# Mask lists copied on chip, values loaded alone, weight loads tied to GpSimd: one change to an mLSTM and mixture-of-experts kernel

## The chip, the cores and the metric

The kernel runs on one core of a Trainium2 chip. The metric is the device time of one launch in microseconds. The time before is the median of three runs. One more execution was recorded by the hardware profiler; every row below comes from it.

## What is computed

Two layers follow each other. The first is a recurrent attention (mLSTM) over 4 batches, 8 heads, 768 positions and 40 features per head; the second sends its output, as 3072 tokens of 320 features, through eight experts with four slots each.

```python
# first layer, for each position t
m_new = maximum(f_gate[t] + m, i_gate[t])
f_stab, i_stab = exp(f_gate[t] + m - m_new), exp(i_gate[t] - m_new)
C = f_stab * C + i_stab * outer(v[t], k[t])
n = f_stab * n + i_stab * k[t]
y[t] = sigmoid(o_gate[t]) * (C @ q[t]) / maximum(abs(n . q[t]), 1)

# second layer, x = y as 3072 x 320
logits = x @ phi                                  # 3072 x 32
d = softmax(logits, over tokens);  c = softmax(logits, over slots)
slot_input = d.T @ x                              # 8 experts x 4 slots x 320
slot_out[e] = maximum(slot_input[e] @ w1[e], 0) @ w2[e]
out = c @ slot_out
```

## The kernel before, in words

The sequence is cut into 6 chunks of 128 positions. A step is one chunk of one batch, so there are 24 steps, ordered chunk by chunk; four steps of one chunk are a group. Everything is written out in program order: each engine executes its instructions in exactly the order in which the code issues them, and waits on semaphores where a tile is not ready. All transfers are issued on SyncE (SP), in one queue, in program order too; a transfer that has to wait for its tile holds back every later one.

For each step the kernel makes three things on TensorE. `expo` (L271 in chunk 0, L273 later) builds the exponents of the decay between all pairs of positions as a product of two lists: `LB` on the left and `RB` on the right, 128 partitions each. Partitions 0 to 63 and those with ones are the fixed part of a list (a triangular mask and selectors); 12 partitions of RB and 24 of LB hold the gate sums of the chunk. There are two buffers of each, one for odd chunks and one for even ones. ScalarE then takes the exponential (L279) and copies the last column as the keys' decay `rl` (L282). `scores` (L293) multiplies queries and keys, `qc` (L307) multiplies queries with the state C, and ScalarE copies that out of its bank as `qs` (L310). `pv` (L363) multiplies decayed scores with values and `state` (L345, L346) decayed keys with values. Banks are scarce: `qc` and `state` share the single bank `ps`, so the products of `state` wait until `qs` is copied.

GpSimd scales the state (`decay_c`, L325), the keys (`keys`, L331: the keys' decay), the outputs (`gate`, L392, tile x) and qs (`decay_q`, L319). VectorE multiplies decay and scores (`mix`, L298) and prepares the denominators (L380 to L383). TensorE turns x (`xtr`, L409), and with some lag the logits and slot sums of finished groups are accumulated.

The loop body of step i issues work ahead: `load_kv(i + 3)`, `load_w1`, `load_wave`, `expo(i + 2)`, `scores(i + 1)`, `qc(i + 1)`, `load_qk(i + 4)`, `keys(i + 1)`, `gate(i - 1)`, `decay_q(i + 1)`, `pv(i)`, `state(i)`. A KV tile holds the keys (320 columns) and the values with a constant column (328). The keys are used by `keys`, which returns at once from step 20 on, since the state after the last chunk isn't needed. No KQ or KV is loaded by steps 21 and 22, no KQ by step 20.

The gate sums of chunks 2 to 5 are worked out in steps 0 to 3, a few operations a step (`emit(rest, RP[i])`, at the end of a step). In step 2 these are L204 and L205 on VectorE, the cast L215 on ScalarE and L216 on GpSimd; in step 3 the cast L217 on ScalarE and L218 on GpSimd. They are then written to memory (`put_gates`, step 4) and read back into the lists (`get_gates`). The fixed part of the odd lists is loaded at the start by `static(1)`, that of the even ones by `static(0)` in step 2.

The weights of the experts come as 20 blocks of w1 (128 x 1024, 512 KB), one a step from step 3 on, and 16 waves of w2 (128 x 4 x 320, 640 KB). A wave goes into tiles of the first layer that are no longer used: wave 0 in step 21, waves 1 and 2 in step 22, the rest behind the loop, as the tiles come free. `W1N` and `W2N` give the numbers by step. In step 21 GpSimd also clears the tiles for the slots (`slT`, `hT`, L640). Behind the loop `up` (L719) multiplies the slots with w1 and `down` (L745) with w2, wave by wave; `combine` (L763) writes the output.

Of the kernel before, what the change touches and what calls it, by code (L numbers as in the profile page):

```python
# [14 lines left out]
B, H, S, D = 4, 8, 768, 40  # L15
# [3 lines left out]
NSTEP = B * NCH  # L19
DM = H * D  # L20
# [3 lines left out]
GRP = B  # L24
# [27 lines left out]
NKV = 4  # L52
NKQ = 3
NX = 7
NWARM = 9
W1N = (0, 0, 0, 1, 1, 1, 1, 1, 1, 1, 1, 1, 1, 1, 1, 1, 1, 1, 1, 1, 1, 1, 1)
W2N = {21: 1, 22: 2}
KT = 128 // 2
KG = KT + 3 * B
# [7 lines left out]
def kernel(ctx: ExitStack, tc: tile.TileContext, qk, kv, og, g0, g1, g2, masks, consts, cr, cl, w1, w2, *outs):  # L67
# [3 lines left out]
    V, A, G, T = nc.vector, nc.scalar, nc.gpsimd, nc.tensor  # L71
# [6 lines left out]
    def pmt(shape, name, tag="pm"):  # L78
        return pp.tile(shape, F32, tag=tag, name=name, bufs=2 if tag == "pm" else 1)

    def load(dst, src):
        nc.sync.dma_start(dst, src)  # L82
# [12 lines left out]
    KV = [KV2[n // 2][:, n % 2] for n in range(NKV)]  # L95
    KQ_ = [sb.tile([P, 1280], F32, tag=f"KQ{n}", name=f"KQ{n}") for n in range(NKQ)]
    KQ = [t[:, 0:1024].rearrange("p (u j t) -> p u j t", u=2, j=4) for t in KQ_]
    RB = [sb.tile([P, 2, 4, L], BF16, tag=f"RB{n}", name=f"RB{n}") for n in range(2)]
    LB = [sb.tile([P, 2, B, L], BF16, tag=f"LB{n}", name=f"LB{n}") for n in range(2)]
# [34 lines left out]
    w1_sb, w2_sb, run = {}, {}, {}  # L134
    NL = NSTEP - 1

    def load_qk(i):
        if i < NSTEP:
            load(KQ[i % NKQ], qk[i])

    def load_kv(i):
        if i < NSTEP:
            load(KV[i % NKV], kv[i])

    def load_sig(gi, u):
        if gi < NGRP:
# [4 lines left out]
    def load_w1(n=1):  # L151
        for _ in range(n):
            k = len(w1_sb)
            if k < 20:
                w1_sb[k] = sb.tile([P, 4 * DM if k == 0 else FF], F32, tag=f"w1_{k}", name=f"w1_{k}")[:, 0:FF]
                load(w1_sb[k], w1v[:, k, :])

    waves = [("w2r0", 1), ("w2r1", 1), ("w2r2", 1), ("sig", 2), ("KQ0", 1), ("KQ1", 1), ("KV0", 1), ("ew", 3),
# [2 lines left out]
    def load_wave(n=1):  # L161
        for _ in range(n):
            w = len(w2_sb)
            tag, bufs = waves[w]
            t = sb.tile([P, 4, DM], F32, tag=tag, name=f"w2_{w}", bufs=bufs)
            load(t, w2[w])
            w2_sb[w] = [t[:, j] for j in range(4)]
# [10 lines left out]
    def static(n):  # L178
        load(RB[n].rearrange("p r j t -> p (r j t)"), cr)
        load(LB[n].rearrange("p a b s -> p (a b s)"), cl)  # L180
# [6 lines left out]
    def gates_of(lo, hi):  # L187
        t, o = (gf1, L) if lo < 2 * L else (gf2, 2 * L)
        return t[:, 0, lo - o:hi - o], t[:, 1, lo - o:hi - o]
# [36 lines left out]
    def put_gates(c0, c1):  # L226
        for u in range(2):
            load(W[u, 3 * c0 - 3:3 * c1 - 3].rearrange("q r t -> r q t"),
                 gp[32 * u:32 * u + 32, c0 - 1:c1 - 1].rearrange("p c q t -> p (c q) t"))

    def get_gates(c):
        if c >= NCH:
            return
        n = c % 2
        load(RB[n][KT:KG].rearrange("p r j t -> p (r j t)"), W[0, 3 * c - 3:3 * c].rearrange("q (b h) t -> (q b) (h t)", b=B))
        load(LB[n][KG:KA].rearrange("p a b s -> p a (b s)"),
             W[1, 3 * c - 3:3 * c].rearrange("q (h b) t -> (q h) (b t)", b=B).unsqueeze(1).broadcast_to([3 * H, 2, B * L]))

    def turn_g(c0, c1):
        pd = pmt([P, c1 - c0, 2, NS], f"pdec{c0}")  # L240
        for c in range(c0, c1):
            x = gates_of(c * L, c * L + L)[1][0:NS]
            T.transpose(pd[:, c - c0, 0], x, ident[0:NS, 0:NS])
            T.matmul(pd[:, c - c0, 1], x[:, L - 1:L].broadcast_to([NS, P]), ident[0:NS, 0:NS], start=True, stop=True)
        A.activation(dec[:, c0 - 1:c1 - 1], pd, AF.Exp)
# [54 lines left out]
    def qc(i):  # L300
        if i < B or i >= NSTEP:
            return
        t, b = KQ[i % NKQ], i % B
        pqs[i] = pq = pp.tile([P, 4, 2, V1], F32, tag="ps", name=f"pq{i}")
        for j in range(4):
            for a in range(2):
                T.matmul(pq[64 * a:64 * a + 64, j].rearrange("p u d -> p (u d)"), t[:, 0, j, 64 * a:64 * a + 64],  # L307
                         C_[:, b, j].rearrange("p u d -> p (u d)"), start=True, stop=True)
        qs[i] = sb.tile([P, 4, 2, V1], F32, tag="qs", name=f"qs{i}", bufs=2)
        A.copy(qs[i], pq)  # L310
# [16 lines left out]
    def keys(i):  # L327
        if i >= NSTEP - B:
            return
        t = kr[i] = KR[i % 2]  # L330
        G.tensor_tensor(  # L331
            t[:, 24:24 + DM].rearrange("p (j r d) -> p j r d", j=4, r=2),
            KV[i % NKV][:, 0:DM].rearrange("p (j r d) -> p j r d", j=4, r=2),
            rl[i].rearrange("p r j -> p j r").unsqueeze(3).broadcast_to([P, 4, 2, D]), ALU.mult)
# [135 lines left out]
    def exp_e():  # L470
        A.activation(run["e"], run["e"], AF.Exp)
# [34 lines left out]
    def sigm(gi):  # L506
        if gi < NGRP:
            A.activation(sig[gi], sig[gi], AF.Tanh, scale=0.5)
# [31 lines left out]
    for i in range(NSTEP - 1):  # L540
        gm, ph_ = divmod(i - 1, GRP)
        gm -= 1
        live = gm >= 0
        if i == 0:
            load_qk(3)
        load_kv(i + 3)
        if i == 0:
            put_gates(1, 2)
            get_gates(1)
        if i == 2:  # L550
            static(0)
        if i == 4:
            put_gates(2, NCH)
            get_gates(2)
        if i % GRP == 2 and i > 2:
            get_gates(i // GRP + 2)
        if i < len(W1N):
            load_w1(W1N[i])
        load_wave(W2N.get(i, 0))

        expo(i + 2)
        if live and ph_ == 1:
            ex_dT(gm)
        if live and ph_ == 2:
            exp_e()
        if live and ph_ == 3:
            comb_hi()
        decay_c(i)
        scores(i + 1)
        qc(i + 1)  # L570
        load_qk(i + 4)
        if i % GRP < 2:
            load_sig(i // GRP + 1, i % GRP)
        if i % GRP == 3:
            sigm(i // GRP + 1)
        keys(i + 1)
        gate(i - 1)
        decay_q(i + 1)
        if i == NL - 1:
            run["x23"] = sb.tile([P, DM + 1], F32, tag="dec", name="x23")  # L580
            G.memset(run["x23"][:, DM:DM + 1], 1.0)
        mix(i + 1)
        if live and ph_ == 2:
            norm_e(gm)
        if live and ph_ == 3:
            comb_lo(G)
        pv(i)
        state(i)
        if i == 0:
            A.activation(sig[0][:, 0], sig[0][:, 0], AF.Tanh, scale=0.5)  # L590
        if i == 1:
            A.activation(sig[0][:, 1:], sig[0][:, 1:], AF.Tanh, scale=0.5)
        if live and ph_ == 0:
            pl = pmt([P, P], f"pl{gm}")
            logits_mm(gm, pl, range(GRP))
            ex_lt(gm, pl)
        if live and ph_ == 1:
            if i == NL - 1:
                pv(NL, "ps")
                psT = pp.tile([P, 2, 512], F32, tag="psc", name="psT")  # L600
                peT = pp.tile([P, 2, 512], F32, tag="pe", name="peT")
            turn_d(gm)
            xtr(i - 1)
            if i < NL - 1:
                pd = pmt([P, GRP, NS], f"pd2{gm}")
                T.transpose(pd.rearrange("p j s -> p (j s)"), run["lt"], ident)
        if live and ph_ == 2:
            psl = slots(gm)
        ops = post_ops(i)
        emit(ops, int(i >= B))  # L610
        carry(i)
        emit(ops)
        if live and ph_ == 0:
            emit(top_ops(gm, run["lt"]))
        if live and ph_ == 1 and i < NL - 1:
            emit(e0_ops(gm, pd))
        if live and ph_ == 2:
            add_slots(gm, psl)
        if i == NL - 1:
            gate(NL - 1)  # L620
            emit(post_ops(NL))
            for h0 in (0, 4):
                gate(NL, V, h0, h0 + 4)
        if not (live and ph_ == 1):
            xtr(i - 1)
        if live and ph_ == 3:
            comb_h(gm, comb_T(pmt([P, GRP, P], f"pc{gm}")))
        if i < len(RP):
            emit(rest, RP[i])
        if i == 0:  # L630
            G.tensor_copy(run["identr"], ident)
        if i == 1:
            turn_g(1, 2)
        if i == 4:
            turn_g(2, NCH)
        if i == NL - 2:
            slT = [sb.tile([P, n, 4, 32], F32, tag=t, name=f"slT{n}") for n, t in ((2, "kr0"), (3, "kr1"))]
            hT = [sb.tile([P, 2, 2, 4, 32], F32, tag=t, name=f"hT{t}") for t in ("RB0", "RB1", "LB0", "LB1")]
            for t in slT + hT:
                G.memset(t, 0.0)  # L640
# [42 lines left out]
    a = sb.tile([P, 1], F32, tag="a", name="a")  # L683
# [238 lines left out]
```

## Time and profile before

| | us |
|---|---|
| median of three runs | 170.7 |
| lowest and highest run | 169.46, 171.03 |
| the profiled execution, its own time | 168.17 |
| its span, first to last instruction | 166.4 |

The span is shorter than the time by what lies around it. A row of the timeline gives start, duration, engine, line, operation, tiles and count; in square brackets stands how long the engine was idle before it and what ended that. L82 is the helper by which every transfer is issued. PEld is TensorE's weight load, which overlaps its matmuls.

### The profile page before, as it was taken

To read this page: it belongs to the slowest core of one execution; us is meant where nothing else is said; L and a number is where in the kernel's file an instruction comes from. 1 tells how busy PE (TensorE), PEld (TensorE's weight loads), DVE (VectorE), ACT (ScalarE), POOL (GpSimd) and SP (SyncE) were. 2 spreads that over 40 slices of the span, in tenths; PEclk is the share of its full clock that TensorE was granted. 3 is DMA by queue.
4 is the path that set the end of the run, shared out by engine and by line. 5 is a ranking of instruction groups with operands and counts; after the bars stand their busy time and mean duration, and the time that the engine had idled before them with its cause. 6 is when DMAs were issued, how large, how long until landed. Compare 5 with 4: busy or idle time off the path is not lost.

```text
span 166.4 us, 6610 instructions
## 1 busy us (share of the span) xinstructions
PE 152.1 (91%) x2755; PEld 119.4 (72%) x2755; DVE 115.2 (69%) x286; ACT 84.9 (51%) x174; POOL 74.1 (45%) x119
## 2 busy tenths in 40 slices
PE   7798999699999999999999999998998999899940
PEld 2486878588887978887998778877885533488610
DVE  5916689925869978899689978898577654323560
ACT  4937373954367565575467754565443401203550
POOL 4005293776564666667645686345391021000000
PEclk9999999959999999999999999999999999999996
DMA  3999659994999999999999999999999999605794
GB/s 100 289 338 305 255 184 318 401 364 83 332 405 357 401 401 373 350 318 331 313 280 360 344 313 357 336 349 297 368 419 407 415 415 417 282 9 197 257 342 160
DMA packets 18498, 52.16 MB, mean 313 GB/s; under 512 B 3064, under 2 KB 3752, under 8 KB 18468
## 3 DMA queue, kind: packets, MB, share of 16 engines
q1 hardware_dynamic: 18468, 51.73, 86.3%
q8 instruction: 22, 0.36, 0.9%
q14 instruction: 8, 0.07, 0.1%
HBM read 47.55 MB, written 4.18 MB: 311 GB/s over the span
## 4 chain that ended last, share of the span: by engine, by line
PE 74%; POOL 6%; issue 5%; DMA 4%; DVE 4%; SPq 2%; ACT 2%; POOLq 0%; DVEq 0%; ACTq 0%
PE psc L293 14%; PE ph L363 11%; PE pq L307 9%; PE phh L719 5%; PE pe L273 5%; PE pt L409 4%; DMA cst<-in_consts_dram 4%; PE psT L745 3%; PE pst L345 3%; PE po L763 3%; SPq L82 2%; PE pl L415 2%; PE peT L745 2%; PE psl L452 2%; POOL E L504 1%
## 5 line engine op out<-in xcount | busy, mean ns | idle before, releaser
L298 DVE TENSOR_TENSOR ew<-psc,ew 128x1024 f32<-128x1024 f32 x24 | 29.3, 1222 | 12.4 <-PE psc L293 11.8
L293 PE MATMUL psc<-KQ 64*128 64x128 f32 x384 | 29.5, 296 | 1.5 <-DMA KQ<-in_qk_dram 0.9
L293 PEld LDWEIGHTS psc<-KQ 64*128 64x128 f32 x384 | 24.7, 197 | 7.5 <-issue 2.6
L279 ACT ACTIVATE ew<-pe 128x1024 f32<-128x1024 f32 x23 | 23.5, 1024 | 6.1 <-PE pe L271 4.3
L363 PE MATMUL ph<-KV,ew 128*64 128x41 f32 x768 | 26.4, 230 | 0.0
L363 PEld LDWEIGHTS ph<-KV,ew 128*64 128x64 f32 x768 | 25.0, 140 | 0.4
L319 POOL TENSOR_TENSOR qs<-qs,dec 128x328 f32<-128x328 f32 x20 | 14.8, 742 | 20.0 <-ACT qs L310 18.0
L392 POOL TENSOR_TENSOR x<-sig,den 128x320 f32<-128x320 f32 x23 | 16.6, 721 | 12.5 <-DVE sig L383 10.9
L331 POOL TENSOR_TENSOR kr<-KV,rl 128x320 f32<-128x320 f32 x20 | 15.2, 759 | 10.2 <-ACT rl L282 10.2
L410 ACT COPY xT<-pt 128x384 f32<-128x384 f32 (+1 forms) x24 | 11.3, 469 | 12.7 <-PE pt L409 11.9
L307 PE MATMUL pq<-C,KQ 128*64 128x82 f32 x320 | 16.4, 246 | 0.0
L307 PEld LDWEIGHTS pq<-C,KQ 128*64 128x64 f32 x320 | 13.0, 140 | 2.5 <-ACT ew L279 0.2
L409 PE MATMUL pt<-cst,x 128*128 128x128 f32 x72 | 12.9, 287 | 1.6 <-POOL x L392 1.1
L386 DVE TENSOR_TENSOR ph<-ph,qs 128x328 f32<-128x328 f32 x19 | 9.6, 505 | 6.5 <-PE ph L363 6.2
L345 PE MATMUL pst<-KV,kr 128*64 128x41 f32 x160 | 12.9, 230 | 1.2 <-ACT qs L310 1.2
L310 ACT COPY qs<-pq 128x328 f32<-128x328 f32 x20 | 8.6, 432 | 7.9 <-PE pq L307 7.6
L273 PE MATMUL pe<-RB,LB 128*128 128x256 bf16 x80 | 12.1, 273 | 0.0
L345 PEld LDWEIGHTS pst<-KV,kr 128*64 128x64 f32 x160 | 11.0, 138 | 1.4 <-ACT qs L310 1.3
L409 PEld LDWEIGHTS pt<-cst,x 128*128 128x128 f32 x72 | 7.7, 141 | 5.8 <-issue 2.3
L325 POOL TENSOR_TENSOR C<-C,dec 104x328 f32<-104x328 f32 x16 | 11.9, 742 | 0.0
L381 DVE SCALAR_TENSOR_TENSOR den<-den 128x8 f32<-128x8 f32 x24 | 10.4, 432 | 0.8
L356 DVE TENSOR_TENSOR C<-pst,C 64x164 f32<-64x164 f32 (+1 forms) x32 | 10.4, 325 | 0.2
(170 smaller groups left out, 249.8 us busy)
## 6 DMA issues: line engine op xcount, KB each, us to landing
KQ<-in_qk_dram SPq DMA_DIRECT2D x24, 512.0 KB, 5.7
w<-in_w_dram SPq DMA_DIRECT2D x20, 512.0 KB, 7.0
w<-in_w_dram SPq DMA_DIRECT2D x16, 640.0 KB, 12.4
KV<-in_kv_dram SPq DMA_DIRECT2D x24, 324.0 KB, 6.5
out_dram<-ob SPq DMA_DIRECT2D x15, 256.0 KB, 4.0
sig<-in_og_dram SPq DMA_DIRECT2D x10, 320.0 KB, 6.3
RB<-in_cr_dram SPq DMA_DIRECT2D x2, 256.0 KB, 7.9
LB<-in_cl_dram SPq DMA_DIRECT2D x2, 256.0 KB, 7.7
```

The lines of the kernel that those rows point to most:

```text
L273: T.matmul(pe[r][:, :, t0:t0 + HL], LB[c % 2][:, a, b], RB[c % 2][:, r, :, t0:t0 + HL], start=True, stop=True)
L279: A.activation(ew[i], pe_, AF.Exp)
L293: T.matmul(psc[:, r, j], t[r0:r1, 1, j], t[r0:r1, 0, j], start=True, stop=True)
L298: V.tensor_tensor(ew[i], pscs.pop(i), ew[i], ALU.mult)
L307: T.matmul(pq[64 * a:64 * a + 64, j].rearrange("p u d -> p (u d)"), t[:, 0, j, 64 * a:64 * a + 64], C_[:, b, j].rearrange("p u d -> p (u d ...
L319: (e or G).tensor_tensor(qs[i], qs[i], dec_of(i, 0).broadcast_to([P, 4, 2, V1]), ALU.mult)
L325: G.tensor_tensor(c, c, dec_of(i, 1, 104).broadcast_to([104, 4, 2, V1]), ALU.mult)
L331: G.tensor_tensor(t[:, 24:24 + DM].rearrange("p (j r d) -> p j r d", j=4, r=2), KV[i % NKV][:, 0:DM].rearrange("p (j r d) -> p j r d", j=4 ...
L345: T.matmul(pst[0:64, j], t[:, 80 * j:80 * j + 64], vc[:, 2 * j], start=True, stop=True)
L363: T.matmul(ph[64 * a:64 * a + 64, h], w[:, h % 2, h // 2, 64 * a:64 * a + 64], vc[:, h], start=i < NL or h == 0, stop=i < NL)
L392: (e or G).tensor_tensor(x_of(i)[:, h0 * D:h1 * D].rearrange("p (h d) -> p h d", d=D), s1_of(i)[:, h0:h1], dens[i][:, h0:h1].unsqueeze(2). ...
L409: T.transpose(pt[:, q, :], x[:, o:o + P], ident)
```

## The change

Six edits. (1) Steps 20 to 23 load only the value columns of KV. (2) `static(0)` is no longer loaded; ScalarE copies the whole odd RB list to the even one at the end of step 1, and LB at the end of step 2. (3) `load_w1` moves from ahead of `expo` to behind `keys(i + 1)`. (4) In front of each of the 20 loads GpSimd writes one column of the tile, and the load, which overwrites that column, has to wait for it; in GpSimd's order this write stands behind `keys(i + 1)` and ahead of `gate(i - 1)`. (5) `load_qk` and `load_sig` now stand behind that load. (6) `load_wave` of a step comes before its `load_w1`.

```diff
     def load_kv(i):
         if i < NSTEP:
-            load(KV[i % NKV], kv[i])
+            k = 0 if i < NSTEP - B else DM
+            load(KV[i % NKV][:, k:], kv[i][:, k:])
...
                 w1_sb[k] = sb.tile([P, 4 * DM if k == 0 else FF], F32, tag=f"w1_{k}", name=f"w1_{k}")[:, 0:FF]
+                if k < sum(W1N):
+                    G.memset(w1_sb[k][:, 0:1], 0.0)
                 load(w1_sb[k], w1v[:, k, :])
...
-        if i == 2:
-            static(0)
         if i == 4:
             put_gates(2, NCH)
             get_gates(2)
         if i % GRP == 2 and i > 2:
             get_gates(i // GRP + 2)
-        if i < len(W1N):
-            load_w1(W1N[i])
         load_wave(W2N.get(i, 0))
...
         scores(i + 1)
         qc(i + 1)
+        if i % GRP == 3:
+            sigm(i // GRP + 1)
+        keys(i + 1)
+        if i < len(W1N):
+            load_w1(W1N[i])
         load_qk(i + 4)
         if i % GRP < 2:
             load_sig(i // GRP + 1, i % GRP)
-        if i % GRP == 3:
-            sigm(i // GRP + 1)
-        keys(i + 1)
         gate(i - 1)
         decay_q(i + 1)
...
         if i == 4:
             turn_g(2, NCH)
+        if i in (1, 2):
+            x, y = (RB, LB)[i - 1]
+            A.copy(x.rearrange("p a b s -> p (a b s)"), y.rearrange("p a b s -> p (a b s)"))
```

## Rows read from the trace of the kernel before

**Rows 1.** The page: TensorE's busy share, and its granted clock in 40 slices.

```profile
PE 152.1 (91%) x2755; PEld 119.4 (72%) x2755; DVE 115.2 (69%) x286; ACT 84.9 (51%) x174; POOL 74.1 (45%) x119
...
PEclk9999999959999999999999999999999999999996
```

**Rows 2.** Waits: engine, tile, line, waited for; us in total, times, longest.

```profile
POOL x L392 <- DVE sig L383: 10.9, 13, 1.6
...
PEld psc L293 <- DMA KQ<-in_qk_dram: 1.9, 1, 1.9
...
SPq L82 <- DMA w<-in_w_dram: 10.2, 11, 1.3
```

**Rows 3.** Timeline of ScalarE, start to 32 us.

```profile
3.61 1.04 ACT L183 COPY RR<-msk 64x1024 f32<-64x1024 f32 x1 [1.39 <-DMA msk<-in_masks_dram]
...
26.76 0.59 ACT L354 COPY C<-pst 64x164 f32<-64x164 f32 x2 [1.32 <-PE pst L346]
...
29.34 0.62 ACT L215 CAST gp<-gf 64x512 bf16<-64x512 f32 x1 [1.49 <-DVE gf L205]
29.87 1.01 ACT L279 ACTIVATE ew<-pe 128x1024 f32<-128x1024 f32 x1
...
31.07 0.42 ACT L310 COPY qs<-pq 128x328 f32<-128x328 f32 x1
31.41 1.27 ACT L508 ACTIVATE sig<-sig 128x1280 f32<-128x1280 f32 x1
```

**Rows 4.** Timeline of TensorE's matmuls, 31 to 45 us.

```profile
31.55 0.25 PE L345 MATMUL pst<-KV,kr 128*64 128x41 f32 x1 [1.21 <-ACT qs L310]
...
32.61 0.55 PE L409 MATMUL pt<-cst,x 128*128 128x128 f32 x3 [0.40 <-POOL x L392]
...
33.53 1.83 PE L293 MATMUL psc<-KQ 64*128 64x128 f32 x16
...
40.56 1.16 PE L293 MATMUL psc<-KQ 64*128 64x128 f32 x16
...
44.92 0.60 PE L273 MATMUL pe<-RB,LB 128*128 128x256 bf16 x4
```

**Rows 5.** Half microseconds: engines' busy us, then clock, DMA share, GB/s.

```profile
33.50:34.00 0.50, 0.50 (x7) 0.47 (x8) 0.00 (x0) 0.50 (x2) 0.00 (x0) 0.84 1.02 408
...
37.00:37.50 0.50, 0.50 (x20) 0.50 (x16) 0.00 (x0) 0.13 (x1) 0.50 (x2) 0.75 0.45 129
```

**Rows 6.** Timeline of SP's transfers, 25 to 117 us.

```profile
25.06 1.03 SPq L82 DMA_DIRECT2D LB<-in_cl_dram  x1
...
39.73 0.32 SPq L82 DMA_DIRECT2D LB<-W  x1
...
111.30 5.57 SPq L82 DMA_DIRECT2D w<-in_w_dram  x8
```

**Rows 7.** Longer stretches, columns as in rows 5.

```profile
111.00:124.50 13.50, 12.78 (x266) 10.79 (x259) 9.70 (x25) 6.55 (x14) 7.91 (x14) 1.00 0.97 355
124.50:146.00 21.50, 19.77 (x241) 10.23 (x241) 11.68 (x46) 5.68 (x16) 2.71 (x6) 1.00 0.94 381
...
128.00:132.00 4.00, 3.89 (x65) 2.41 (x64) 2.32 (x8) 1.76 (x7) 0.00 (x0) 1.00 1.03 419
...
145.00:146.00 1.00, 1.00 (x24) 0.56 (x16) 0.30 (x1) 0.00 (x0) 0.00 (x0) 1.00 0.14 56
```

**Rows 8.** Timeline of GpSimd, 31 to 125 us.

```profile
31.85 0.71 POOL L392 TENSOR_TENSOR x<-sig,den 128x320 f32<-128x320 f32 x1
...
115.56 0.73 POOL L504 TENSOR_TENSOR E<-e,E 128x256 fp32r<-128x256 f32 x1
...
121.94 0.99 POOL L640 MEMSET hTLB<- 128x512 f32 x2
...
124.58 0.10 POOL L581 MEMSET x<- 128x1 f32 x1
```

**Rows 9.** Timeline of TensorE, the second half of the first down block.

```profile
146.84 1.93 PE L745 MATMUL psT<-w,hTLB 128*32 128x128 f32 x64
```

More of the change, by code (lines that the diff above doesn't have):

```diff
@@ L55 @@
 NWARM = 9
-W1N = (0, 0, 0, 1, 1, 1, 1, 1, 1, 1, 1, 1, 1, 1, 1, 1, 1, 1, 1, 1, 1, 1, 1)
+W1N = (0, 0, 0, 1, 1, 1, 1, 1, 1, 1, 1, 1, 1, 1, 1, 1, 1, 1, 1, 1, 1, 1, 1, )
 W2N = {21: 1, 22: 2}
```

## The prediction

> **What bounds the kernel now.** I read the page first. TensorE is busy for 91% of the span, and its granted clock is at the upper level in all slices but one [rows 1]: so the question for every edit is whether it starts a TensorE instruction earlier or later. Next the list of waits. In it TensorE waits for a transfer only once, 1.9 us for a KQ load before 12 us, ahead of anything the change touches; no matmul waits for KV, for a mask list or for a weight. SP's longest wait for a transfer is another one: 11 times, 10.2 us in all, it waits for earlier weight loads [rows 2]. That is how the weights look when the queue is full, and it costs nothing until a matmul needs a weight that is late. Then the timelines, engine by engine, in the two places where the change acts: steps 1 to 4 (about 20 to 41 us) and the handover from the loop to the expert stage (111 to 149 us).
>
> In steps 2 to 4 the reader is to see one chain. VectorE finishes the decay lists of the later chunks late, so ScalarE stands idle for 1.49 us in front of the cast of L215 (29.34 us), then does the exponentials of step 5 (29.87) and only then the copy of qs (31.07) [rows 3]. TensorE's state product of step 3 (L345) needs the bank which that copy empties: it waits 1.21 us, to 31.55; then its transposes wait 0.40 us more, for GpSimd's x, to 32.61 [rows 4]. About 1.2 us later the clock falls to its lower level and stays there from about 33.8 to 37.2 us, through the score block at 33.53 (1.83 us, where the same block takes 1.16 at 40.56) [rows 4, 5].
>
> **The mask copies.** Removed: two loads of 256 KB; the second takes SP 1.03 us to issue, at 25.06 us [rows 6]. What SP issues next (KQ and KV of step 6) gets out a good 1 us sooner and, at the 419 GB/s of a pure stream [rows 7], finds 0.52 MB = 1.3 us less ahead of it. But the first matmul on it is the score block at 40.56 us [rows 4], 14 us behind that issue: worth nothing.
> Added: two ScalarE copies of 128x1024 bf16. No such copy is in the trace. Nearest is the f32 copy of the same length, 1.04 us; the lower end is the 512-element cast, 0.62 us; the upper end is the 1280-element tanh at 31.41, 1.27 us [rows 3]. I take 1.04, the row with the same count of elements. (The Trainium skill, "ScalarE: Activation LUTs", What ACT_TABLE_LOAD costs, gives 186 ns and 0.833 ns an element, fp32 and bf16 alike: 1.04 us as an estimate. It speaks against hoping that bf16 halves the copy; the trace agrees for f32.)
> - The RB copy stands behind L245 at the end of step 1. It pushes the exponentials behind it by at most its own 1.04 us; ScalarE then has 1.32 us idle in front of L354 at 26.76 [rows 3]. Hidden: 0. Without that cover it would cost up to 1.04.
> - The LB copy stands at the end of step 2 in program order, behind L215. So it can't use the 1.49 us of idle time in front of L215, and it lies before the exponentials and the qs copy: qs goes from 31.07 to 32.1, L345 from 31.55 to 32.58. The 0.40 us that TensorE loses now in front of its transposes is swallowed: L345's group takes 0.66 us (32.61 - 0.40 - 31.55), so they start at 32.58 + 0.66 = 33.24 instead of 32.61 [rows 4]. **Cost 1.03 - 0.40 = 0.63 us** (bounds: 0.62 - 0.40 = 0.2, and 1.27 - 0.40 = 0.9).
> Late next: the second cast (L217) moves by up to 1.03 us, GpSimd's L218 behind it too, and with it x of step 3; if TensorE then has to wait for this x, that is at most 1.03 - 0.63 = 0.4 us more. The lists of chunk 2, which come out of L218, are issued at 39.73 now and would be at about 40.8; their first matmul is at 44.92 and would be at 45.55 [rows 4, 6]: 4.7 us are left to them of 5.2, and I count nothing.
>
> **The held weights.** Twenty memsets of one column on GpSimd, each 0.10 us by the one at L581 [rows 8], behind the keys' decay and ahead of x. Cover: x waits 13 times, 10.9 us in all, for VectorE [rows 2], some 0.8 us a step. So 0; if the cover were gone, 20 x 0.1 = 2 us at most, and not below nothing, since nothing that TensorE waits for is moved forward by it. The new wait is on SP: behind a held weight stand that step's KQ load, the og load and the next step's KV load. In a steady step the keys' decay ends before the last qc matmul, for which the KQ load waits anyway, so only the weight itself moves, by about 1 us. In step 3 the memset comes where x starts now, at 31.85 [rows 8]; the KQ load behind it goes out at about 32.4, for a score block behind the 44.92 of rows 4: nothing.
>
> **The end of the loop** is where this wait bites. In steps 20 to 22 SP has run ahead of the other engines: now it issues eight weight loads in a row from 111.30 to 116.9 [rows 6], and eleven more as the queue and the tiles let them out. With the hold, w1 block 17 goes out after GpSimd's work of step 19, block 18 after that of step 20 (L504 ends at 116.3), and block 19 only after GpSimd's memsets of step 21 (122.9) [rows 8]. All w2 waves from number 3 stand behind block 19. From 122.95 (123.6 with the 0.63) there are 13 waves of 640 KB and one block of 512 KB to move: 9.04 MB. In the trace 381 GB/s x 21.5 us = 8.19 MB were moved from 124.5 to 146.0 [rows 7], and 124.5 is about when the first byte after 122.95 can flow. 0.85 MB more at 419 GB/s is **2.0 us later for the last wave**. Now the stream thins out to 56 GB/s in 145 to 146 and is then over [rows 7]: the last wave would be there at about 148.0 to 148.5, in old time. It is needed for the last eighth of the block that runs from 146.84 for 1.93 us: 148.4, or somewhat before [rows 9]. The engines' lag of one behind the other should shrink, as the queue runs dry just before 123 and all 16 start together; I take half a microsecond to a whole one of slack, and a cost of 0 (bounds: 0, and 1.5 by the rival below).
>
> **Values alone.** Four KV loads lose 160 KB each: 0.66 MB, 1.6 us of the queue at 419 GB/s, in steps 17 to 20. No matmul waits for KV, and the queue drains during the hold of steps 20 to 22 in any case: 0.
>
> **Sum.** 0.63 us on 168.17 (span 166.4 and 1.8 around it) is 168.8: +0.4%. The runs' median is 170.7, 1.5% above the profiled execution, so 171.3 on their scale.
>
> **The rivals.**
> A, the last waves come too late (slower). Mechanism, place and price: block 19 held to 123, and TensorE waiting at the second half of the first down block. It decides at the rate: from 123.6 + 1.5 to 149.0, with 1 us for the slowest of the 16 engines, there are 22.9 us for 9.04 MB, so below 395 GB/s it waits. For: the whole stretch from 111 to 124.5 ran at 355 [rows 7]; 9.04 MB at that rate take 25.5 us, 2.6 late by this sum, some 1.5 if the slowest engine costs nothing. Against: the pure weight stream holds 419. Time: 171.3 + 1.5 = 172.8. (The Trainium skill, "DMA: Bandwidth & Descriptors", Specifications, puts HBM for one core at 358 GB/s, which would land on the same side; this trace's 419 contradicts it.)
> B, the longer stall keeps the clock low for longer (slower). One low spell of 3.4 us at half clock costs 1.7 us now; a second one after a gap of 2.2 us instead of 1.2 adds as much: 171.3 + 1.7 = 173.0. For: the fall follows the gap. Against: the page has one such fall in the whole span [rows 1], and the matmuls that follow the gap are as dense as before.
> C, transfers do bound the timed runs (faster). These are up to 2.9 us slower than the profiled execution; if late loads are the reason, 1.18 MB less is worth up to 2.8 us: 168.5. Against: the one execution with rows has not a single wait of this kind.
> D, the hold does nothing, since SP would have waited anyway, and the LB copy is as short as 0.62 us: 170.7 + 0.2 = 170.9.
>
> **How the numbers follow.** Forecast 0.48, A 0.17, B 0.10, C 0.12, D 0.13. The forecast's own range is 170.2 to 172.3, its bounds of 0.2 to 0.9 and the 0.5% by which the shown runs stray. Forecast and D lie within 1%, about what a measurement of this kernel can tell from no change; A and B lie on its edge or past it (172.4), and a few of their cases fall inside: faster 0.12, same 0.65, slower 0.23. The range from 169.3 to 173.4 leaves out most of C and the far ends of A and B.
>
> **What would show it.** Right: two bf16 copies of about 1.04 us on ScalarE near 24 and 29.9; L345's wait for qs about 2.2 us; the score block of 33.53 some 0.6 us later; block 19 issued right after GpSimd's memsets of step 21; no TensorE wait for w. Wrong: a wait for w at L745, a second low stretch of the clock, or step 4 no later than now.

## The result and the profile after

The changed kernel takes 172.3 us in the median of 20 runs (169.65 to 175.74), the kernel before, on the same chips, 170.6 (20 runs, 168.15 to 173.5). The ratio is 1.0114, with a 95% interval of 1.0069 to 1.0159. The forecast was 171.3, or +0.4%, in a range of 169.3 to 173.4. So the time lies in the range, but the likeliest case was too mild: by the ratio the loss is about 1.9 us and not 0.6. Disturbed runs are left out of all ratios here; of the four profiled executions that were such runs, that of the first experiment (mean clock 0.76) isn't read, and those of three repeats (1.0110, 1.0041 and 1.0108 below) are read for single rows alone.

The page of the profiled execution of the changed kernel (span 170.2 us, its own time 172.01; its line numbers are three or four higher than in the rows of before, those of the experiments none to four):

```profile
PE 151.4 (89%) x2755; PEld 117.7 (69%) x2755; DVE 114.3 (67%) x286; ACT 87.0 (51%) x176; POOL 74.9 (44%) x139
...
PEclk9999999879999999999999999999999999999995
```

Set beside [rows 1], TensorE does the same 2755 matmuls in nearly the same busy time, and the clock has one dip in the loop, as before. So the 3.8 us of longer span are idle time of TensorE. The waits of the changed kernel say where two of the gaps are (engine, tile, line, waited for; us in all, times, longest):

```profile
POOL x L395 <- DVE sig L386: 11.2, 14, 1.5
...
PE pst L348 <- ACT qs L313: 2.2, 1, 2.2
...
PE psT L749 <- DMA w<-in_w_dram: 1.0, 1, 1.0
```

The second row is the wait of steps 2 and 3, which was 1.21 us. The last is new: a TensorE wait for w, the row that the prediction named as the sign that it was wrong. One more wait is in no row of before, at the first matmul of chunk 1:

```profile
23.20 0.60 PE L276 MATMUL pe<-RB,LB 128*128 128x256 bf16 x4 [0.89 <-DMA LB<-W]
```

It isn't put down to the change: of the experiments below, the copies alone and the hold in the middle alone, which share no edit, have it too (0.78 and 0.66 us), while the hold at the end alone and the copies with LB twice do not. SP issues this list at 21.46 us, in the trace before at 21.38; TensorE came there earlier in this execution (x's transposes just ahead start at 21.36, before at 22.60). The timeline of ScalarE in the changed kernel shows both copies:

```profile
22.68 1.04 ACT L639 COPY RB<-RB 128x1024 bf16<-128x1024 bf16 x1
...
29.04 0.62 ACT L218 CAST gp<-gf 64x512 bf16<-64x512 f32 x1 [1.48 <-DVE gf L208]
29.57 1.04 ACT L639 COPY LB<-LB 128x1024 bf16<-128x1024 bf16 x1
30.51 1.01 ACT L282 ACTIVATE ew<-pe 128x1024 f32<-128x1024 f32 x1
```

The LB copy stands where it was predicted, behind the cast and behind 1.48 us of idle time that it can't use. The exponentials start 1.47 us after the cast, where in [rows 3] they start 0.53 after it: 0.94 us more. Then TensorE's timeline, in three places:

```profile
32.20 0.25 PE L348 MATMUL pst<-KV,kr 128*64 128x41 f32 x1 [2.15 <-ACT qs L313]
...
32.90 0.90 PE L412 MATMUL pt<-cst,x 128*128 128x128 f32 x3
...
54.04 0.20 PE L348 MATMUL pst<-KV,kr 128*64 128x41 f32 x1 [0.91 <-issue]
...
73.47 0.26 PE L366 MATMUL ph<-KV,ew 128*64 128x41 f32 x3 [0.42 <-issue]
...
148.84 1.85 PE L749 MATMUL psT<-w,hTLB 128*32 128x128 f32 x56
151.72 0.43 PE L749 MATMUL psT<-w,hTLB 128*32 128x128 f32 x8 [1.03 <-DMA w<-in_w_dram]
```

At 32 us the wait grew from 1.21 to 2.15 us and the 0.40 us of waiting for x is gone, both as the prediction had them [rows 4]. In the loop two gaps end on "issue", that is on nothing which the profile shows. At 149 the first down block, one group of 64 without a pause in [rows 9], breaks after 56 matmuls, and its last eighth waits 1.03 us for the last w2 wave. Why that wave is late is told by SP, by GpSimd and by the stretches of the DMA queue. First SP of the changed kernel, then GpSimd:

```profile
125.06 0.33 SPq L82 DMA_DIRECT2D w<-in_w_dram  x1
125.49 1.64 SPq L82 DMA_DIRECT2D w<-in_w_dram  x1
```

```profile
124.00 0.99 POOL L644 MEMSET hTLB<- 128x512 f32 x2
124.93 0.10 POOL L158 MEMSET w<- 128x1 f32 x1
```

Block 19 is issued right behind GpSimd's one-column write, which stands right behind the memsets of step 21, as predicted. The next load is the first of the deferred waves, and it took 1.64 us to issue. Then the stretches (busy us of the engines, then clock, DMA share, GB/s) of the changed kernel:

```profile
125.06:130.00 4.94, 4.11 (x80) 3.29 (x77) 3.90 (x12) 1.66 (x4) 2.22 (x4) 1.00 0.72 216
130.00:149.00 19.00, 18.09 (x248) 9.35 (x251) 9.65 (x39) 4.47 (x13) 1.88 (x3) 1.00 1.01 413
149.00:150.00 1.00, 1.00 (x48) 1.00 (x40) 0.00 (x0) 0.00 (x0) 0.00 (x0) 1.00 0.40 149
150.00:151.00 1.00, 0.69 (x21) 0.25 (x12) 0.00 (x0) 0.00 (x0) 0.00 (x0) 1.00 0.16 67
151.00:152.00 1.00, 0.28 (x12) 0.28 (x16) 0.00 (x0) 0.00 (x0) 0.00 (x0) 1.00 0.09 22
```

For five microseconds after block 19 the queue moves only 216 GB/s. Then it holds 413, about the 419 that the prediction reckoned with, and runs out in a tail of 149, 67 and 22 GB/s, with TensorE partly idle in the last two rows. The prediction had the full rate from the start.

The theory at this point: the LB copy costs about what was forecast, and the hold at the end of the loop, put down as hidden, costs a microsecond or more. The rivals: that the clock or the gaps ending on "issue" make up the rest, or that the hold in the middle of the loop does.

### The profile page after: what moved, and what is told of

Its sections match the earlier page's. It is cut to its first block, busy times and chain, and to the rows that moved or that the text cites. A ratio compares the mean times of both kernels' runs of the same rounds, so it can differ in the third digit from the quotient of the medians.

```text
span 170.2 us, 6650 instructions
## 1 busy us (share of the span) xinstructions
PE 151.4 (89%) x2755; PEld 117.7 (69%) x2755; DVE 114.3 (67%) x286; ACT 87.0 (51%) x176; POOL 74.9 (44%) x139
## 4 chain that ended last, share of the span: by engine, by line
PE 66%; DMA 10%; POOL 6%; issue 6%; DVE 3%; SPq 2%; ACT 2%; POOLq 0%; DVEq 0%; ACTq 0%
PE psc L296 13%; PE ph L366 10%; PE pq L310 8%; DMA w<-in_w_dram 6%; PE pe L276 5%; PE pt L412 4%; DMA cst<-in_consts_dram 4%; PE pst L348 3%; PE phh L723 3%; PE po L767 3%; SPq L82 2%; PE pl L418 2%; PE peT L749 2%; PE psl L455 2%; POOL kr L334 1%
## 5 line engine op out<-in xcount | busy, mean ns | idle before, releaser
L296 PE MATMUL psc<-KQ 64*128 64x128 f32 x384 | 28.9, 290 | 1.3 <-DVE ew L301 0.9
L296 PEld LDWEIGHTS psc<-KQ 64*128 64x128 f32 x384 | 24.1, 192 | 7.7 <-issue 2.8
L366 PEld LDWEIGHTS ph<-KV,ew 128*64 128x64 f32 x768 | 24.7, 138 | 0.9 <-issue 0.5
L395 POOL TENSOR_TENSOR x<-sig,den 128x320 f32<-128x320 f32 x23 | 16.6, 722 | 11.9 <-DVE sig L386 11.2
L310 PE MATMUL pq<-C,KQ 128*64 128x82 f32 x320 | 15.8, 240 | 0.0
L310 PEld LDWEIGHTS pq<-C,KQ 128*64 128x64 f32 x320 | 12.5, 136 | 2.4
L386 DVE SCALAR_TENSOR_TENSOR sig<-sig,ph 128x320 f32<-128x320 f32 x24 | 10.5, 438 | 0.0
```

What stands on the lines that cost most here:

```text
L296: T.matmul(psc[:, r, j], t[r0:r1, 1, j], t[r0:r1, 0, j], start=True, stop=True)
L366: T.matmul(ph[64 * a:64 * a + 64, h], w[:, h % 2, h // 2, 64 * a:64 * a + 64], vc[:, h], start=i < NL or h == 0, stop=i < NL)
L395: (e or G).tensor_tensor(x_of(i)[:, h0 * D:h1 * D].rearrange("p (h d) -> p h d", d=D), s1_of(i)[:, h0:h1], dens[i][:, h0:h1].unsqueeze(2). ...
```

## The experiments

**The hold at the end, taken out of the changed kernel.** Blocks 17 to 19, the only ones issued when SP has run ahead, lose their one-column write and go out at once:

```diff
-                if k < sum(W1N):
+                if k < 17:
                     G.memset(w1_sb[k][:, 0:1], 0.0)
```

> The changed kernel, with GpSimd's column write ahead of w1 blocks 0 to 16 only: blocks 17 to 19, and with them the w2 waves, no longer wait for GpSimd in steps 20 to 22. Theory 1 (the hold at the end of the loop and the LB copy are the loss): TensorE's wait for w at the end of the first down block, 1.03 us in the changed kernel, is gone, and the ratio to the kernel before falls from 1.011 to about 1.004, what the LB copy leaves. Theory 2 (the loss sits in the middle of the loop, where TensorE stood 0.91 and 0.42 us with no releaser shown, and comes from weight loads bunched by the hold): the wait for w goes but the gaps without releaser stay, and the ratio stays at 1.008 or more. If the end is no part of the loss: 1.011 as before.

Measured: 1.0025 of before (0.9972 to 1.0078). By this alone nearly all of the loss was the hold at the end; two repeats below weaken that.

**The hold at the end, alone.** The kernel before, with the weight loads moved behind the keys as in the change, and the write ahead of blocks 17 to 19 only:

```diff
+                if 17 <= k < 20:
+                    G.memset(w1_sb[k][:, 0:1], 0.0)
...
-        if i < len(W1N):
-            load_w1(W1N[i])
...
+        keys(i + 1)
+        if i < len(W1N):
+            load_w1(W1N[i])
         load_qk(i + 4)
...
-        keys(i + 1)
```

> The kernel before, with the w1 load moved behind the keys' decay as in the change, and GpSimd's column write ahead of blocks 17 to 19 alone; lists loaded, KV whole. Theory 1: block 19 is issued right behind GpSimd's memsets of step 21 (about 123 us), the last w2 wave lands about 2 us later than before, TensorE waits 0.5 to 1.5 us for it; ratio 1.003 to 1.009. Theory 2: nothing, 1.000, with or without a wait for w, and no gap without releaser.

Measured: 1.0090 (1.0041 to 1.0139). TensorE's timeline in this kernel:

```profile
37.52 0.55 PE L411 MATMUL pt<-cst,x 128*128 128x128 f32 x3 [0.95 <-POOL x L394]
...
146.75 1.49 PE L747 MATMUL psT<-w,hTLB 128*32 128x128 f32 x48
149.06 0.43 PE L747 MATMUL psT<-w,hTLB 128*32 128x128 f32 x8 [0.81 <-DMA w<-in_w_dram]
150.52 0.43 PE L747 MATMUL psT<-w,hTLB 128*32 128x128 f32 x8 [1.04 <-DMA w<-in_w_dram]
```

The last group starts at 146.75, where [rows 9] has 146.84, so the two waits, 1.85 us together, are the price of the hold in this execution. (The first row, a wait in step 4 for x of step 3, is taken up at the end of the experiments.) SP's rows are those of the changed kernel again: block 19 at 122.95, the wave behind it at 123.39, 1.77 us to issue. The stretches of this kernel let the failed sum be redone, since block 19 goes out at the very time that the prediction took:

```profile
124.50:128.00 3.50, 2.67 (x29) 1.86 (x25) 2.83 (x11) 1.27 (x4) 0.82 (x2) 1.00 0.71 251
128.00:146.00 18.00, 17.09 (x214) 8.36 (x217) 8.81 (x36) 4.44 (x13) 1.88 (x3) 1.00 1.02 411
146.00:147.00 1.00, 1.00 (x44) 1.00 (x41) 0.84 (x4) 0.00 (x0) 0.00 (x0) 1.00 1.06 421
147.00:148.00 1.00, 1.00 (x48) 0.97 (x36) 0.00 (x0) 0.00 (x0) 0.00 (x0) 1.00 0.48 184
148.00:149.00 1.00, 0.24 (x12) 0.00 (x0) 0.00 (x0) 0.00 (x0) 0.00 (x0) 1.00 0.25 97
149.00:150.00 1.00, 0.43 (x8) 0.19 (x8) 0.00 (x0) 0.00 (x0) 0.00 (x0) 1.00 0.08 31
150.00:151.00 1.00, 0.48 (x19) 0.48 (x23) 0.00 (x0) 0.00 (x0) 0.00 (x0) 1.00 0.06 16
```

Rate times length, row by row, is 0.88 + 7.40 + 0.42 + 0.18 + 0.10 + 0.03 + 0.02 = 9.03 MB: the 9.04 MB of the prediction were right. The same first stretch in the trace of the kernel before, and two rows of its tail (the one between them is in [rows 7]):

```profile
124.50:128.00 3.50, 2.68 (x31) 1.87 (x28) 2.90 (x11) 1.22 (x3) 0.84 (x3) 1.00 1.02 412
...
144.00:145.00 1.00, 1.00 (x36) 0.70 (x28) 0.45 (x1) 0.00 (x0) 0.00 (x0) 1.00 0.34 138
...
146.00:147.00 1.00, 1.00 (x41) 1.00 (x44) 0.88 (x4) 0.00 (x0) 0.00 (x0) 1.00 0.03 10
```

There the queue is full; here it has to fill again. The difference, 161 GB/s for 3.5 us, is 0.56 MB, or 1.4 us of the stream. So by this sum the last waves came 2.0 + 1.4 = 3.4 us later. The DMA packets in the two traces agree: the last one of w2 ends at 146.51 us before and at 150.04 here, 3.5 us later. The tail tells nothing of the hold: the last 0.4 MB took 2.9 us before, 3.0 here and 2.5 in the changed kernel. And the last eight matmuls of the block start 0.5 us after the last packet: 150.52 after 150.04 here, 151.72 after 151.24 in the changed kernel.

**The copies alone.** The kernel before, with `static(0)` removed and both copies as in the change:

```diff
-        if i == 2:
-            static(0)
...
+        if i in (1, 2):
+            x, y = (RB, LB)[i - 1]
+            A.copy(x.rearrange("p a b s -> p (a b s)"), y.rearrange("p a b s -> p (a b s)"))
```

> The kernel before with the second fixed lists copied on ScalarE as in the change, and nothing else. Theory 1: L345's wait for qs grows from 1.2 to 2.2 us, the following score block starts 0.6 us later against the one of step 2, no wait for w; ratio 1.002 to 1.006. Rival (two loads of 256 KB fewer are worth as much as the copy costs): 0.998 to 1.001. Rival (the longer stall brings a second low stretch of the clock): 1.010 or more, with more than one stretch of 3.4 us at half clock in the profile.

Measured: 1.0051 (0.9997 to 1.0105), which is 0.9 us with a bound just below nothing. TensorE's timeline in this kernel:

```profile
32.65 0.25 PE L345 MATMUL pst<-KV,kr 128*64 128x41 f32 x1 [2.16 <-ACT qs L310]
...
33.41 0.90 PE L409 MATMUL pt<-cst,x 128*128 128x128 f32 x3
```

The gap is 2.16 us, with no wait for x behind it and no wait for w at the end of the kernel. The copies are enough to make the gap grow.

**The LB copy twice.** As the copies alone, with the LB copy written twice, to see whether it stands on the path with its full length:

```diff
+        for n in (1, 2, 2):
+            if i != n:
+                continue
+            x, y = (RB, LB)[n - 1]
+            A.copy(x.rearrange("p a b s -> p (a b s)"), y.rearrange("p a b s -> p (a b s)"))
```

> The kernel before with the lists copied on ScalarE as in the change, the LB copy written twice, one behind the other at the same place; no hold, KV whole. Theory 1 (what stands ahead of the qs copy there comes straight onto TensorE's path): L345's wait grows by another copy, 0.94 to 1.04 us, to 3.1 or 3.2 us, and the ratio is one such step (0.55 to 0.6%) above the one of the copies alone: about 1.011. Rival (TensorE's clock decides and makes up for part of it): within 0.2% of the copies alone, 1.003 to 1.007. Rival (a longer gap brings a second low stretch): 1.016 or more, and more than one stretch of 3.4 us at half clock.

Measured: 1.0155 (1.0108 to 1.0202). ScalarE's timeline, then TensorE's, in this kernel:

```profile
29.37 2.12 ACT L638 COPY LB<-LB 128x1024 bf16<-128x1024 bf16 x2
```

```profile
33.08 0.25 PE L345 MATMUL pst<-KV,kr 128*64 128x41 f32 x1 [3.24 <-ACT qs L310]
```

1.21, 2.16, 3.24 us with none, one and two copies: each copy adds its length to the gap. In time the second adds 1.04% (1.0155 against 1.0051, from two sets of runs), some 1.8 us, for 1.08 us of gap; the intervals are too wide to say that the rest is anything. There was one low stretch of the clock in the loop, as in the trace before.

**The copies put into the idle time, no hold.** Values alone, `static(0)` removed, and the copies of steps 1 and 2 ahead of the instructions of step 2 in which ScalarE waits for VectorE:

```diff
+        if i in (1, 2):
+            x, y = (RB, LB)[i - 1]
+            A.copy(x.rearrange("p a b s -> p (a b s)"), y.rearrange("p a b s -> p (a b s)"))
         if i < len(RP):
             emit(rest, RP[i])
```

> The kernel before with values alone in the last four steps and the lists copied on ScalarE, but both copies issued ahead of that step's share of the gate sums, so that the LB copy can run while ScalarE waits for VectorE (1.49 us idle in the profile of before); no hold, w1 loads where they were. Theory 1: both copies are hidden, L345's wait is 1.2 us as before, no wait for w; ratio 0.997 to 1.001. If transfers were what the timed runs lose (rival C of the prediction): 0.985 to 0.992. If the copies cost wherever they stand: 1.003 to 1.006.

Measured: 0.9972 (0.9924 to 1.0020). Repeated in another set of runs:

> The covered copies with values alone and no hold once more, for its interval (0.9924 to 1.002 the first time). Theory 1: 0.997 to 1.001, no wait for w, L345's wait 1.2 us. If transfers bound the timed runs (rival C): below 0.992.

Measured: 1.0041 (0.9990 to 1.0092). The first execution's timelines, ScalarE and then TensorE:

```profile
27.90 1.05 ACT L629 COPY LB<-LB 128x1024 bf16<-128x1024 bf16 x1
29.48 0.62 ACT L216 CAST gp<-gf 64x512 bf16<-64x512 f32 x1 [0.53 <-DVE gf L206]
```

```profile
31.70 0.25 PE L346 MATMUL pst<-KV,kr 128*64 128x41 f32 x1 [1.21 <-ACT qs L311]
```

The copy takes 1 us out of ScalarE's idle time, which shrinks from 1.49 to 0.53, and the gap is back at 1.21. So the same copy costs TensorE nothing where it stands ahead of the wait. By time the two readings lie on both sides of 1: this version isn't shown to beat the kernel before, and neither the values alone nor the saved 512 KB of lists bring a gain that shows.

**The hold in the middle, alone.** As the hold at the end alone, but for blocks 0 to 16:

```diff
+                if k < 17:
+                    G.memset(w1_sb[k][:, 0:1], 0.0)
```

> The kernel before with the w1 load moved behind the keys' decay and GpSimd's column write ahead of blocks 0 to 16 alone (steps 3 to 19); lists loaded, KV whole. Theory 1: no engine waits longer than before, no wait for w at the end; ratio 0.997 to 1.003. Theory 2 (the hold bunches the weight loads in the loop, and TensorE's gaps without releaser come from it): such gaps of 0.9 us and more in the loop, ratio 1.005 to 1.010.

Measured: 1.0023 (0.9972 to 1.0074), with the gap at 1.20 us and no wait for w. In this kernel, too, one gap ends on "issue":

```profile
104.21 0.94 PE L295 MATMUL psc<-KQ 64*128 64x128 f32 x11 [1.09 <-issue]
```

**The changed kernel again,** for what its first profile had by chance:

> The changed kernel once more, for a second profile and beside the others on one chip. Theory 1: the wait for w at the end of the first down block is there again, 0.8 us or more, and L345's of about 2.2 us; ratio 1.008 to 1.016. The gaps without releaser, 0.91 and 0.42 us in the first profile at 54 and 73 us, lie elsewhere or are absent, if they are chance (theory 2: they are at the same places).

Measured: 1.0110 (1.0046 to 1.0174), the first result again. TensorE's timeline:

```profile
32.32 0.25 PE L348 MATMUL pst<-KV,kr 128*64 128x41 f32 x1 [2.15 <-ACT qs L313]
...
47.91 1.13 PE L366 MATMUL ph<-KV,ew 128*64 128x41 f32 x32 [0.29 <-issue]
...
150.68 0.43 PE L749 MATMUL psT<-w,hTLB 128*32 128x128 f32 x8 [1.14 <-DMA w<-in_w_dram]
```

Both waits are back to a tenth of a microsecond. The gaps that end on "issue" are not: 0.29 us in another place. They belong to the execution: every other one that can be read has between none and three of them, 0.2 to 1.1 us long, and that of before has none.

**An attempt at the gap itself.** Values alone, no hold, and two of the instructions behind the late lists moved from step 2 to step 3, with the LB copy at the end of step 3; then the same with both copies at the end of step 1:

```diff
-    RP = (2, 3, 4, 2)
+    RP = (2, 3, 2, 2)
...
         qc(i + 1)
+        if i == 3:
+            emit(rest, 1)
...
         decay_q(i + 1)
+        if i == 3:
+            emit(rest, 1)
```

> Values alone and lists copied, no hold, and the gap itself taken away: the cast L215 moves from the end of step 2 behind the qs copy of step 3, L216 on GpSimd behind that step's work on qs, and the LB copy to the end of step 3. ScalarE then no longer waits for VectorE ahead of the qs copy. Theory 1: L345's wait of 1.2 us goes, and with it the 0.4 us for x; if the fall of the clock hangs on that gap, the low stretch of 3.4 us goes too: 1.6 us without the clock, 3.3 with it, ratio 0.981 to 0.992. Rival (the lists of chunk 2 come late instead and the first matmul of chunk 2 waits for them): 0.995 to 1.005, with a wait for LB or RB near 45 us. Rival (the gap only moves to the next step): 0.994 to 1.0.

Measured: 1.0011 (0.9963 to 1.0060). The wait for qs moved one step on:

```profile
36.55 0.25 PE L346 MATMUL pst<-KV,kr 128*64 128x41 f32 x1 [1.50 <-ACT qs L311]
```

> As the run with the gap of step 3 removed, but with both list copies at the end of step 1, into ScalarE's 1.3 us of idle time there, since that run showed the LB copy at the end of step 3 making a new gap of 1.50 us in step 4 and a late fall of the clock. Theory 1: L345's waits of step 3 and step 4 are together below 0.7 us; ratio 0.988 to 0.996 if the clock still falls once, 0.978 to 0.988 if it doesn't. Rival (the gap goes to yet another step, or the double copy delays the exponentials of step 2): 0.996 to 1.002, with a gap of 1 us or more between 25 and 45 us.

Measured: 1.0116 (1.0070 to 1.0162). The wait for qs shrank and a wait for x took its place:

```profile
35.79 0.25 PE L346 MATMUL pst<-KV,kr 128*64 128x41 f32 x1 [0.80 <-ACT qs L311]
...
37.61 0.55 PE L410 MATMUL pt<-cst,x 128*128 128x128 f32 x3 [1.16 <-POOL x L393]
```

In both the dip of the clock came later too, at 39 to 44 us. The lists of the later chunks have to be made somewhere in these steps, and in both orders TensorE waited 1.2 to 1.5 us there for another engine; neither order is a gain.

**The hold at the end taken out, again, twice.** The first reading decides how much of the loss is the hold, so it was repeated in two further sets of runs:

> The changed kernel without the hold on blocks 17 to 19 once more, as its first profile was taken in a disturbed execution. Theory 1: L345's wait about 2.15 us, no wait for w at the end of the first down block, the last wave landed by about 146 to 147 us; ratio 1.002 to 1.006. Rival (the end is no part of the loss): 1.010.

Measured: 1.0108 (1.0064 to 1.0153). Beside these runs the kernel before stands low, with a median of 168.8 against 170.4 and 169.6 in other sets, and the three ratios taken against it stand high: this one, and 1.0041 and 1.0116 above.

> The changed kernel without the hold on blocks 17 to 19 a third time, since its two ratios, 1.0025 and 1.0108, lie apart by more than their intervals. Theory 1 (the LB copy alone is left): 1.002 to 1.007, so that the mean of three stays below the changed kernel's 1.011. Rival (the end is no part of the loss): 1.009 or more.

Measured: 1.0088 (0.9978 to 1.0198), an interval that is wide because only two runs of the kernel before go into it. The page and TensorE's timeline of this execution (span 165.9 us):

```profile
PEclk9999999999999999999999999999999999999999
```

```profile
32.60 0.25 PE L348 MATMUL pst<-KV,kr 128*64 128x41 f32 x1 [2.16 <-ACT qs L313]
...
38.64 0.55 PE L412 MATMUL pt<-cst,x 128*128 128x128 f32 x3 [1.21 <-POOL x L395]
...
147.03 1.93 PE L749 MATMUL psT<-w,hTLB 128*32 128x128 f32 x64
```

Without the hold the block of 64 runs through in one piece, and so it does in the execution of the second reading (149.93, 1.93 us, x64).

And here a gap of 2.16 us is followed by no dip of the clock at all. That saves less than the 1.7 us which a dip costs by itself, as the second row shows: TensorE now comes to x's transposes of the next step too early and waits 1.21 us for GpSimd. In the trace before, with its dip, they start without a wait:

```profile
38.29 0.55 PE L409 MATMUL pt<-cst,x 128*128 128x128 f32 x3
```

The hold alone had no dip either, and waits 0.95 us at the same place. From the end of the gap to these transposes there are 6.74 us before (31.55 to 38.29) and 6.18 in the hold alone (31.34 to 37.52); with the longer gap there are 6.24 in the changed kernel (32.20 to 38.44) and 6.04 here. So a dip at this place costs 0.2 to 0.6 us, since GpSimd's x takes back most of what a full clock would give. The span of 165.9 us, half a microsecond below that of before, is no gain of the steps looked at here: TensorE's block starts 0.19 us later than in [rows 9].

## Why the prediction came out as it did

- **The mask copies: right, place and size.** Forecast 1.04 us a copy and 0.63 us net. Measured 1.04 us for both; the gap grew by 0.94 us and swallowed x's 0.40 us. In the first profile TensorE came to the gap 0.29 us earlier than in the trace before and began x's transposes 0.29 us later (32.90 against 32.61), so 0.58 us net. The copies alone read +0.5% (0.0 to 1.1). The sign given for it was off: the score block of 33.53 starts 1.05 us later and not 0.6 (34.58): the clock is low from 32.6 us on, and the transposes ahead of it take 0.90 us instead of 0.55. But in step 4 the score block of 40.56 starts at 40.71. And "late next" had its reason: in the two executions without a dip TensorE waits for x of step 3, 1.21 us with the copy and 0.95 without, 0.26 more, within the 0.4 that was allowed.
- **The memsets and the hold in the loop: right, nothing that shows.** 0.10 us each in front of x, which still waits for VectorE 14 times and 11.2 us, against 13 and 10.9 [rows 2]. Alone they read 1.0023 with 1 well inside the interval.
- **Values alone: right as far as it can be told.** They were not run by themselves; in what was run no gain shows, so rival C falls: the two readings without hold and with covered copies have a mean of 1.0007, where C asked for 0.987.
- **The end of the loop: the failed step, by size.** Place, order and bytes were as forecast, and in the hold alone the issue time too. The cost of 0 was wrong: it measured 1.0 to 1.9 us of waiting. Three terms made it. The term "2.0 us later for the last wave" measured 3.5 us, because the sum ran the stream at its full rate from 124.5 us and the restarted queue gave 251 GB/s in its first 3.5 us. The stream was not over at 146.0: its last packet ended at 146.51, and TensorE starts 0.5 us after it, so the spare time was 148.4 - 147.0 = 1.4 us and not 2.4, too little for the 2.0 already. And the guess that the 16 engines' lag would shrink after a common start is not borne out: the last 0.4 MB took 2.9 us before, 3.0 in the hold alone and 2.5 in the changed kernel. The "half a microsecond to a whole one of slack" was not there. (That the first byte needs 1.5 us was too long by 0.5: the first packet of block 19 starts at 123.92 us, 0.97 behind the start of its issue.) That the time still lies in the range is owed to the range, which held part of rival A, not to this step. The three executions with the hold at the end wait 1.03, 1.14 and 1.85 us for w; none of the nine others that can be read, nor that of before, has such a wait. That is rival A, in its place: its line was 395 GB/s, and the rows of the hold alone give 8.90 MB from 124.5 to 148.24, where TensorE stopped with a quarter of the block to do, or 375. Rival D, that the hold does nothing, falls with the same waits. (The Trainium skill, "DMA: Bandwidth & Descriptors", Specifications, has 358 GB/s for one core, which gave the right side for a wrong reason: the steady stream measured 411 to 413 here too.)
- **Rival B: not supported, and its price was too high.** Gaps of 2.15 us came with one dip, as 1.21 did, and in one execution 2.16 came with none. In the second reading without the hold there are two dips, 24.7 to 28.1 and 35.0 to 38.4 us; the first stands behind a gap of 1.28 us for the list of chunk 1, ahead of the gap of step 3 (1.75 us there). So whether a dip comes was not set by the length of this gap alone. And the price of 1.7 us counts the matmuls and not what follows them: measured at x of the next step it is 0.2 to 0.6 us. (The prediction counted one low slice in [rows 1]; the last one, a 6, is low too, but no matmul is left in it.)

What the hold costs in time stays open within bounds. Alone it reads +0.9% (0.4 to 1.4), and its waits of 1.0 to 1.9 us are 0.6 to 1.1% of 170. But the changed kernel without it reads 1.0025, 1.0108 and 1.0088, a mean of 1.0074, against 1.0114 and 1.0110 with it: a difference of 0.4%, or 0.6 us. Single readings stray by more than that, and the kernel before, against which they are taken, strays from set to set too. Set against each other without it, the 15 runs of the changed kernel that go into its two ratios have a mean of 170.8 us, and the 25 without the hold at the end 169.4: 1.4 us apart (0.8 to 2.1), which is what the waits say. These runs come from several chips, so this is a second estimate and no proof. That the wait is there, and that the hold makes it, is shown; that it is the larger of the two costs is likely by the second estimate and not shown by the ratios. Of the 3.8 us between the two profiled spans, 1.3 us are the two gaps that end on "issue" and belong to that one execution: a subtraction of two spans would have put them down to the change.

## What to carry to other kernels

A load that is tied to another engine's order has to be priced where its queue ran furthest ahead, not in a steady step: there the tie drains the queue, and the restart (here 1.4 us of stream) comes on top of the bytes that are late. A copy that replaces a load should stand ahead of the instruction in which its engine already waits: here the place in program order decided between 0.9 us more gap and none. A fall of the clock should be priced where the next wait ends, not by the matmuls that it slows. And before a difference of two spans is explained, the gaps without a releaser should be taken out of it, by a second profile of the same kernel.

## What the hardware showed that was not expected

After a pause the queue did not come back at its full rate: 251 GB/s over 3.5 us in one execution, 216 over 4.9 in another (from the issue on), then 411 to 413. In these two the second load behind the pause took SP 1.77 and 1.64 us to issue, in the repeat of the changed kernel the third, 1.48 us; whether the slow issue holds back the stream or the other way round was not tried. (The Trainium skill, "DMA: Bandwidth & Descriptors", Specifications, gives a first byte after about 0.6 us for such a queue. The traces agree: the first packet of block 19 starts 0.64 us after its issue ends in both executions, at 123.92 after 123.28 and at 126.02 after 125.38. So it isn't the first byte that is late; the 1.4 us of stream lost are more than twice that.)

TensorE's clock fell to its lower level for 3.4 us between 24 and 44 us in most executions, in two of them twice or for twice as long, and in two not at all, one with the longer gap in front and one with the shorter. Each such fall takes up to 1.7 us from the matmuls; measured at the next step, where TensorE has to wait for GpSimd's x, it cost 0.2 to 0.6 us.
